# Sharing the opening loads of a layer-norm, state-space and GeGLU kernel among three issuing engines, and transposing x between the two halves of B

## The chip, the cores and the metric

The kernel runs on one core of a Trainium2 chip. In the profile, TensorE (matrix products, and here transposes too) is PE, its weight loads PEld, VectorE DVE, ScalarE ACT and GpSimd POOL; SyncE (SP) does nothing here but issue transfers (DMA). A q behind a name stands for that engine's sequencer, which here issues transfers or waits. TensorE's results go to PSUM buffers. The metric is the device time of one execution in microseconds (us), as the median of several. Each kernel also has a profile of one execution; its span is some 1.8 us shorter than that execution's time, because the time holds a little more than the instructions. All profiles used here are of fast executions; an execution is called slow when it lies over 1.5% above the fastest of the same kernel. Ratios compare one kernel's fast executions with those of the kernel before in the same rounds, so they are not quite the ratio of the medians that stand beside them. Landing records, and the times of single packets, were read from the trace file itself; they are not among the views shown.

## The reference, cut to what matters

Over 2048 tokens with 512 features: a layer norm, then two branches of the same normalised x, multiplied.

```python
xn = _layernorm(x, axis=-1)
# s: Bu = xn @ B_bar.T (complex B), h = Lam_bar * h + Bu over 2048 steps,
#    y = 2 * Re(h @ C.T) + xn * Dskip
s = _A_ref(xn, Lambda_re, Lambda_im, B_re, B_im, C_re, C_im, log_dt, Dskip)
# g: silu of a feed-forward of width 1376
g = _silu((_gelu(xn @ w_gate) * (xn @ w_up)) @ w_down)
return x + s * g
```

## The kernel before: the parts that matter

The tokens are worked on in four blocks of 512. TensorE needs x and B with the features on the partitions, so both have to be transposed. For block 0 this is done on TensorE at the very start, and that opening is what the change rewrites.

```python
for m in range(M):                                   # M = 4 pieces of x (0 to 3), 128 KB each
    nc.sync.dma_start(out=x_tok[:, m, :], in_=x_r[:, m, :])
for i, v in enumerate((A_log_dt, A_Lambda_im, A_Lambda_re, A_Dskip)):   # 1 KB each
    nc.scalar.dma_start(out=pv[4 * i : 4 * i + 4, :], in_=...)
for ri, src in enumerate((A_B_re, A_B_im)):          # 512 KB each
    nc.sync.dma_start(out=Bn[:, ri, :, :], in_=...)
# ... weights; identity and constants on GpSimd; "tiny", a first Sin on ScalarE ...
dummies(10)                 # matmuls on zeros, meant to have TensorE's clock up
# transpose of the parameters (pt_ps), dummies(3), statistics of x, norms 0 and 1
b_transposes(0)             # 16 transposes, two ScalarE copies
tps = [t_xn0(0, xs[0]), t_xn0(1, xs[1])]
xs += [norm0(2), norm0(3)]
b_transposes(1)
# copies of x's transposes 0, 1; transposes 2, 3; their copies; then the first products, u_ps
```

For blocks 2 and 3 the normalised x is transposed by DMA, one piece of 128 tokens at a time, while TensorE works on the block before. The change does not touch this code, but the explanation needs it:

```python
def ln_out(s, m):
    xn = work.tile([P, D], BF16, name="xn", tag="xn", bufs=4)
    ACT(out=xn[:], in_=x_tok[:, s * M + m, :], func=AF.Identity, ...)
    nc.sync.dma_start_transpose(out=xnT[:, :, c0 : c0 + P], in_=xn[:])
# in step j (of 11) of block s:
if 5 <= j < 5 + M:
    ln_out(s + 1, j - 5)    # the last piece is in step 8; the next block's u_ps follow step 10
```

## Time and profile before

| | kernel before |
|---|---|
| time, median of 3 (range) | 188.81 us (188.59 to 189.18) |
| span of the profile | 187.59 us |
| first product, u_ps of block 0 | 10.35 us |
| last block's first u_ps | 123.40 us |

The page's engine lines and the opening's chain of waits are in the prediction below. Two more things are worth a look. The first is the timeline of the opening (columns: start, length in us, engine, line, operation, tile; in brackets the idle time and what ended it):

```profile
2.94 1.29 DVE L151 BATCH_NORM_STATS2 st<-x_tok 128x6 f32<-128x512 bf16 x2 [1.82 <-DMA x_tok<-in_A_x_dram]
```

VectorE runs the statistics of the first two pieces of x back to back, so both had landed by 3.6. The second is the chain of waits just before the last block (start, length, what):

```profile
119.96 3.31 DMA xnT<-xn
...
123.40 4.69 PE u_ps L333 x21
```

Here the end of the kernel hangs on a transfer: the last piece of block 3's transposed x, issued at 119.96 and landed 3.31 us later.

### The profile page before, as it was taken

What the parts mean: (1) busy time and instruction counts of PE and PEld (TensorE: products, weight loads), DVE (VectorE), ACT (ScalarE), POOL (GpSimd) and SP (SyncE); (2) the same over time, 40 slices, a digit from 0 to 9 for tenths busy, and PEclk for the clock granted to TensorE, in tenths of its full rate; (3) what the DMA queues carried; (4) which work ended last, traced back from release to release, by engine and by line L of the source; (5) the groups of instructions that cost most, each with busy time, mean ns of one, the idle gap of its engine ahead of it and who ended that gap; (6) DMA issues with size and microseconds to landing.
All of it is one profiled execution on the core that took longest, in us unless ns stands there. A gap on an engine that the chain in (4) does not pass through costs nothing.

```text
span 187.6 us, 2592 instructions
## 1 busy us (share of the span) xinstructions
PE 180.8 (96%) x918; PEld 86.0 (46%) x918; DVE 156.0 (83%) x269; ACT 116.2 (62%) x209; POOL 21.2 (11%) x35
## 2 busy tenths in 40 slices
PE   7789999999999999999999999989999999999992
PEld 2644444444444444544444444544444444554452
DVE  4859999999999599999999997999999999332033
ACT  3499899997279969257259947937428733441210
POOL 3745400000000330000000192000000000000000
PEclk9999999999999999999999999999999999999999
DMA  5999968600000013200000001420000000000001
GB/s 145 330 365 361 225 123 246 119 3 0 0 0 0 0 30 86 56 28 28 3 2 0 2 0 42 101 56 28 0 0 0 3 0 28 28 29 31 28 28 58
DMA packets 21164, 12.26 MB, mean 65 GB/s; under 512 B 11456, under 2 KB 21152, under 8 KB 21152
## 3 DMA queue, kind: packets, MB, share of 16 engines
q1 hardware_dynamic: 20976, 12.03, 23.9%
q8 instruction: 7, 0.11, 0.2%
q10 hardware_dynamic: 176, 0.07, 0.1%
q14 instruction: 5, 0.04, 0.1%
HBM read 7.38 MB, written 2.10 MB: 51 GB/s over the span
## 4 chain that ended last, share of the span: by engine, by line
PE 57%; DVE 21%; ACT 10%; DMA 4%; POOL 3%; issue 3%; SPq 1%; POOLq 1%; ACTq 0%; DVEq 0%
PE f_ps L438 15%; PE u_ps L333 11%; PE g_ps L418 10%; PE up_ps L423 10%; PE y_ps L453 6%; DVE Ft L382 6%; ACT junk L508 3%; DVE qq L352 3%; ACT gt L428 3%; ACT ub L430 3%; DVE pp L352 3%; DVE Wt L356 2%; DMA Bn<-in_A_B_re_dram 2%; DMA xnT<-xn 2%; DVE at L431 1%
## 5 line engine op out<-in xcount | busy, mean ns | idle before, releaser
L418 PE MATMUL g_ps<-xnT,wg 128*128 128x512 bf16 (+1 forms) x176 | 45.2, 379 | 0.0
L423 PE MATMUL up_ps<-xnT,wu 128*128 128x512 bf16 (+1 forms) x176 | 45.2, 379 | 0.0
L438 PE MATMUL f_ps<-wd,at 128*128 128x512 bf16 (+1 forms) x176 | 38.7, 379 | 0.0
L428 ACT ACTIVATE gt<-g_ps 128x512 bf16<-128x512 f32 (+1 forms) x44 | 26.0, 592 | 10.0 <-PE g_ps L418 7.8
L382 DVE TENSOR_TENSOR_SCAN Ft<-rho,it,Wt 128x512 bf16<-128x512 f32 x24 | 29.9, 1271 | 0.0
L333 PE MATMUL u_ps<-xnT,BT 128*128 128x512 bf16 x128 | 28.3, 379 | 1.1 <-DVE xnT L212 0.6
L430 ACT ACTIVATE ub<-up_ps 128x512 bf16<-128x512 f32 (+1 forms) x44 | 26.3, 597 | 3.9 <-PE up_ps L423 3.8
L453 PE MATMUL y_ps<-C,hst 128*128 128x512 bf16 x120 | 28.3, 379 | 0.0
L423 PEld LDWEIGHTS <-wu 128*128 128x128 bf16 (+1 forms) x176 | 17.6, 100 | 20.4
L438 PEld LDWEIGHTS <-at 128*128 128x128 bf16 (+1 forms) x176 | 17.2, 98 | 20.6
L443 ACT ACTIVATE g<-f_ps 128x512 f32<-128x512 f32 x16 | 9.6, 597 | 27.1 <-PE f_ps L438 27.1
L418 PEld LDWEIGHTS <-wg 128*128 128x128 bf16 (+1 forms) x176 | 17.2, 100 | 18.4
L431 DVE TENSOR_TENSOR at<-gt,ub 128x512 bf16<-128x512 bf16 (+1 forms) x44 | 18.1, 414 | 7.3 <-ACT ub L430 7.1
L338 ACT ACTIVATE U<-u_ps 128x512 bf16<-128x512 f32 x32 | 17.8, 602 | 9.0 <-PE u_ps L333 9.0
L471 DVE TENSOR_TENSOR yg<-y_ps,g 128x512 bf16<-128x512 f32 x15 | 10.3, 684 | 13.7 <-PE y_ps L458 9.9
L333 PEld LDWEIGHTS <-BT 128*128 128x128 bf16 x128 | 12.3, 98 | 15.9 <-issue 1.4
L453 PEld LDWEIGHTS <-hst 128*128 128x128 bf16 x120 | 11.7, 98 | 13.6
L523 ACT ACTIVATE xn<-x_tok,nb,rs 128x512 bf16<-128x512 bf16 x12 | 9.7, 812 | 5.6 <-POOL nb L519 5.6
L513 POOL TENSOR_SCALAR sx<-sx 128x4 f32<-128x4 f32 x2 | 2.2, 1118 | 82.0 <-ACT junk L508 82.0
L356 DVE TENSOR_TENSOR Wt<-pp,qq 128x1024 bf16<-128x1024 bf16 x16 | 10.6, 688 | 0.3
L356 DVE TENSOR_TENSOR hst<-pp,qq 128x1024 bf16<-128x1024 bf16 x16 | 10.6, 687 | 0.2
L508 ACT ACTIVATE junk<-x_tok 128x512 bf16<-128x512 bf16 x16 | 10.1, 629 | 0.3
(109 smaller groups left out, 163.3 us busy)
## 6 DMA issues: line engine op xcount, KB each, us to landing
out_dram<-ot SPq DMA_DIRECT2D x15, 128.0 KB, 1.7
x_tok<-in_A_x_dram SPq DMA_DIRECT2D x3, 512.0 KB, 3.9
wd<-in_B_w_down_dram SPq DMA_DIRECT2D x1, 1280.0 KB, 10.5
x_tok<-in_A_x_dram SPq DMA_DIRECT2D x4, 128.0 KB, 2.2
Bn<-in_A_B_re_dram SPq DMA_DIRECT2D x1, 512.0 KB
Bn<-in_A_B_im_dram SPq DMA_DIRECT2D x1, 512.0 KB, 5.0
wg<-in_B_w_gate_dram SPq DMA_DIRECT2D x1, 512.0 KB, 9.4
wu<-in_B_w_up_dram SPq DMA_DIRECT2D x1, 512.0 KB
```

The source lines that it names most:

```text
L333: nc.tensor.matmul(u_ps[:, :], lhsT=BT[:, ri, kt, pt * P : (pt + 1) * P], rhs=xnT[:, kt, cols], start=(kt == 0), stop=(kt == KT - 1),)
L338: ACT(out=U[:, ri, q, :], in_=u_ps[:, :], func=AF.Copy)
L356: return lambda: TT(out=dst()[i], in0=box["pp"][:, i, :, :], in1=box["qq"][:, 1 - i, :, :], op=op)
L382: nc.vector.tensor_tensor_scan(out=box["F"][:, ri, q, :], data0=rho[:, pt : pt + 1].to_broadcast([P, TS]), data1=box["W"][:, ri, q, :], in ...
L418: nc.tensor.matmul(g_ps[:fs, :], lhsT=wg[:, kt, fsl], rhs=xnT[:, kt, cols], start=(kt == 0), stop=(kt == KT - 1))
L423: nc.tensor.matmul(u_ps[:fs, :], lhsT=wu[:, kt, fsl], rhs=xnT[:, kt, cols], start=(kt == 0), stop=(kt == KT - 1))
L428: ACT(out=gt[:fs], in_=g_ps[:fs, :], func=AF.Gelu_apprx_tanh)
L430: ACT(out=ub[:fs], in_=u_ps[:fs, :], func=AF.Copy)
L431: dve(now() + 0.9, 0.34, lambda: TT(out=at[:fs, j, :], in0=gt[:fs], in1=ub[:fs], op=ALU.mult))
L438: nc.tensor.matmul(f_ps[:, :], lhsT=at[:fs, k, m0 : m0 + P], rhs=wd[:fs, k, :], start=(k == 0), stop=(k == NFT - 1))
L453: nc.tensor.matmul(y_ps[:, :], lhsT=hst[:, j // NPT, j % NPT, m0 : m0 + P], rhs=C2[:, j // NPT, j % NPT, :], start=(j == 0), stop=False,)
L508: ACT(out=junk[:], in_=x_tok[:, s * M + m, :], func=f, accum_out=sx[:, s, i, m : m + 1])
```

## The change

Its intent: move ScalarE's table load to the front, spread the issues of the opening loads over three engines so that half of B comes sooner, and put the transposes of x where TensorE would wait for B's other half. Core of the diff:

```diff
+    tiny = consts.tile([P, 1], FP32, name="tiny")
+    ACT(out=tiny[:], in_=halfpi[:], func=AF.Sin)          # table load, now first on ScalarE
     for i, v in enumerate((A_log_dt, A_Lambda_im, A_Lambda_re, A_Dskip)):
-        nc.scalar.dma_start(out=pv[4 * i : 4 * i + 4, :], ...)
+        nc.gpsimd.dma_start(out=pv[4 * i : 4 * i + 4, :], ...)
-    for m in range(M): nc.sync.dma_start(out=x_tok[:, m, :], ...)      # (stood above)
-    for ri, src in enumerate((A_B_re, A_B_im)): nc.sync.dma_start(out=Bn[:, ri, :, :], ...)
+    nc.sync.dma_start(out=x_tok[:, 0, :], ...)
+    nc.sync.dma_start(out=x_tok[:, 1, :], ...)
+    nc.sync.dma_start(out=x_tok[:, 2:M, :], ...)
+    load_b(nc.scalar, 0, A_B_re)
+    load_b(nc.sync, 1, A_B_im)
 ...
-    dummies(10)
-    (transpose of the parameters pt_ps, dummies(3), statistics, copy pf, norms 0 and 1,
-     thn, a1, b_transposes(0), x transposes 0 and 1, norms 2 and 3, b_transposes(1))
+    dummies(12)
+    b_transposes(0)
+    (statistics, norms 0 and 1, x transposes 0 and 1, transpose of the parameters pt_ps,
+     b_transposes(1), copy pf, norms 2 and 3)
     (copies of x 0 and 1, x transposes 2 and 3, their copies)
+    (thn, a1)
 ...
-    clk["pe"] = 9.5
+    clk["pe"] = 9.3                                       # start assumed in the VectorE schedule
```

More of the change, by code (lines that the diff above doesn't have):

```diff
@@ L87, with load_b @@
     wu_r = B_w_up.rearrange("(k p) f -> p k f", p=P)
-    for m in range(M):
-        nc.sync.dma_start(out=x_tok[:, m, :], in_=x_r[:, m, :])
-    for i, v in enumerate((A_log_dt, A_Lambda_im, A_Lambda_re, A_Dskip)):
-        nc.scalar.dma_start(out=pv[4 * i : 4 * i + 4, :], in_=v.rearrange("(k p) -> k p", p=P))
-    for ri, src in enumerate((A_B_re, A_B_im)):
-        nc.sync.dma_start(out=Bn[:, ri, :, :], in_=src.rearrange("(k p) d -> p k d", p=P))
+    def load_b(eng, ri, src):
+        eng.dma_start(out=Bn[:, ri, :, :], in_=src.rearrange("(k p) d -> p k d", p=P))
+    halfpi = consts.tile([P, 1], FP32, name="halfpi")
+    nc.vector.memset(halfpi[:], math.pi / 2)
+    tiny = consts.tile([P, 1], FP32, name="tiny")
+    ACT(out=tiny[:], in_=halfpi[:], func=AF.Sin)
+    for i, v in enumerate((A_log_dt, A_Lambda_im, A_Lambda_re, A_Dskip)):
+        nc.gpsimd.dma_start(out=pv[4 * i : 4 * i + 4, :], in_=v.rearrange("(k p) -> k p", p=P))
+    nc.sync.dma_start(out=x_tok[:, 0, :], in_=x_r[:, 0, :])
+    nc.sync.dma_start(out=x_tok[:, 1, :], in_=x_r[:, 1, :])
+    nc.sync.dma_start(out=x_tok[:, 2:M, :], in_=x_r[:, 2:M, :])
+    load_b(nc.scalar, 0, A_B_re)
+    load_b(nc.sync, 1, A_B_im)
     cuts = [0, 3 * P, 7 * P, F]
@@ L107 @@
     nc.vector.memset(warm[:], 0.0)
-    halfpi = consts.tile([P, 1], FP32, name="halfpi")
-    nc.vector.memset(halfpi[:], math.pi / 2)
     ident_f = consts.tile([P, P], FP32, name="ident_f")
@@ L120 @@
     nc.gpsimd.memset(mhalf[:], -0.5)
-    tiny = consts.tile([P, 1], FP32, name="tiny")
-    ACT(out=tiny[:], in_=halfpi[:], func=AF.Sin)
     euler = consts.tile([P, NPT], FP32, name="euler")
@@ L181 @@
     ch = consts.tile(W3, BF16, name="ch")
-    dummies(10)
+    dummies(12)
+    b_transposes(0)
+    for a in (0, 2):
+        for m in (a, a + 1):
+            bn(0, m)
+        for m in (a, a + 1):
+            bn_end(0, m)
+        rstd(0, a, a + 2)
+    xs = [norm0(0), norm0(1)]
+    tps = [t_xn0(0, xs[0]), t_xn0(1, xs[1])]
     pt_ps = psum.tile([P, 16], BF16, name="pt_ps", tag="ps")
     nc.tensor.transpose(pt_ps[:, :], pv[:, :], ident[0:16, 0:16])
-    dummies(3)
-    bn(0, 0)
-    bn(0, 1)
-    bn_end(0, 0)
-    bn_end(0, 1)
-    rstd(0, 0, 2)
-    bn(0, 2)
+    b_transposes(1)
     nc.vector.tensor_copy(out=pf[:], in_=pt_ps[:, :])
     nc.gpsimd.tensor_tensor(out=dt_[:], in0=euler[:], in1=ldt, op=ALU.pow)
-    bn(0, 3)
-    bn_end(0, 2)
-    bn_end(0, 3)
-    rstd(0, 2, 4)
-    xs = [norm0(0), norm0(1)]
-    STT(out=thn[:], in0=lim, scalar=1.0 / (2.0 * math.pi), in1=dt_[:], op0=ALU.mult, op1=ALU.mult)
-    TT(out=a1[:], in0=lre, in1=dt_[:], op=ALU.mult)
-    nc.gpsimd.tensor_tensor(out=rho[:], in0=euler[:], in1=a1[:], op=ALU.pow)
-    b_transposes(0)
-    tps = [t_xn0(0, xs[0]), t_xn0(1, xs[1])]
     xs += [norm0(2), norm0(3)]
-    b_transposes(1)
     for m in range(2):
@@ L212 @@
         nc.vector.tensor_copy(out=xnT[:, :, m * P : (m + 1) * P], in_=tps[m][:, :, :])
+    STT(out=thn[:], in0=lim, scalar=1.0 / (2.0 * math.pi), in1=dt_[:], op0=ALU.mult, op1=ALU.mult)
+    TT(out=a1[:], in0=lre, in1=dt_[:], op=ALU.mult)
+    nc.gpsimd.tensor_tensor(out=rho[:], in0=euler[:], in1=a1[:], op=ALU.pow)
     TT(out=ang[:], in0=iota_f[:].unsqueeze(1).to_broadcast(W3), in1=thn[:].unsqueeze(2).to_broadcast(W3), op=ALU.mult)
```

## The prediction

> **What bounds the kernel now.** I read the page first: TensorE is busy for 96% of the span, so only the places where it is not busy, and the place where it starts, can be worth anything. The page's lines that say so:
>
> ```profile
> PE 180.8 (96%) x918; PEld 86.0 (46%) x918; DVE 156.0 (83%) x269; ACT 116.2 (62%) x209; POOL 21.2 (11%) x35
> PE   7789999999999999999999999989999999999992
> ```
>
> The reader is to see that the thin slices are the first two (4.69 us each) and the last. The change touches only what runs before the first real product, so I read next the chain that ended last, piece by piece, from 0 to 45 us (columns: start, length, what):
>
> ```profile
> 2.18 0.43 SPq L89
> 2.61 0.04 issue
> 2.65 4.07 DMA Bn<-in_A_B_re_dram
> 6.72 0.05 issue
> 6.77 1.07 PE tb_ps L140 x16
> 7.84 0.45 PE tp L171 x8
> 8.28 1.00 PE tb_ps L140 x16
> 9.28 0.24 PE tp L171 x4
> 9.52 0.02 issue
> 9.54 0.77 DVE xnT L212 x2
> 10.31 0.04 issue
> 10.35 7.07 PE u_ps L333 x32
> ```
>
> So the start is a chain: SyncE issues four pieces of x, then the real half of B; that half lands at 6.72; 32 transposes of B and 16 of the normalised x follow, two DVE copies end it, and at 10.35 the first product u_ps starts. From 10.35 to 52.9 the chain is TensorE without a gap. From 52.9 to 123.4 it goes through ScalarE and VectorE work that hangs on a product ending at 52.9, then back to TensorE. No piece of it starts at a fixed time of its own. A start later by d therefore ends the kernel later by about d.
>
> The other direction is not symmetric. The timeline near 36 us:
>
> ```profile
> 29.62 5.22 SPq L525 DMA_TRANSPOSE xnT<-xn  x4
> 36.30 6.59 PEld L333 LDWEIGHTS <-BT 128*128 128x128 bf16 x32 [0.36 <-DMA xnT<-xn]
> ```
>
> The second token block's transposed x arrives just when TensorE wants it: the weight load had sat idle for 0.36 us until that transfer, although TensorE itself ran on. SyncE's queue runs without a pause from 16.9 us (eight transposes of C, two loads of x, then these four), so this arrival is set by transfers. An earlier start gains only as far as the queue is earlier too.
>
> **What the Trainium skill says.** "DMA: Bandwidth & Descriptors", section "Issuing engines are not separate DMA queues": transfers started by ScalarE, SyncE or GpSimd run on the same 16 DMA engines and interleave; several issuers save only issue time. The trace before agrees as to the bound: from 4.4 to 7.2 us the DMA engines moved 349 to 367 GB/s with one queue doing nearly all of it, so a second queue has little left to add. The same page, "Queues, rings and completion order": each DMA engine takes turns between the queues that have work. No trace here shows that, since the second queue carried only 4 KB. "Perfetto Trace Analysis", section "DVE / Act Engine Instruction": an ACTIVATE is pushed into a wait queue, after which the sequencer is free for the next instruction. If a DMA issue runs on that sequencer, it could pass the table load. The trace before cannot settle that: there the four issues came first (until 2.27) and the load at 2.29. "DMA: Bandwidth & Descriptors", section "Anatomy of one DMA — SWDGE (gpsimd) path": a GpSimd transfer has descriptors written by software and about 2 us of fixed cost. No run here has one.
>
> **The change, part by part.**
>
> *ScalarE's table load* starts at about 0.75 instead of 2.29. It takes 1.28 and the first Sin 0.20, and ScalarE's next work was at 7.43: hidden both times, worth 0.
>
> *The loads.* Before, x (0.52 MB) moved until about 3.85, the rate fell to 91 GB/s until 4.40, and B_re followed. It moved by about 5.75 and landed at 6.72, so landing is 0.97 after the last byte. Afterwards SyncE issues three pieces of x (0.46 each, from 0.72) and B_im at about 2.1. If ScalarE's issue of B_re waits for load and Sin, it is at 0.75 + 1.28 + 0.20 = 2.25, only 0.4 earlier than the 2.65 before. B_im was issued 0.15 before it, and the two halves share the engines. Steady data for B_re began some 1.6 after its issue, so both flow from about 3.75. Two halves are 1.05 MB, at 357 GB/s 2.95 us: data until 6.7, landing at 7.65. B_re would be 0.9 later than now, B_im (needed at 8.21 before) 0.5 earlier. The saved issues and the filled dip (0.55 us at 91 instead of 350, about 0.4 us of transfer) go to the second half, which was not the one waited for.
>
> *GpSimd.* Four issues now come ahead of the identity and the constants. I take 1 us each, an estimate from the skill's fixed cost of 2 us, half of it held by GpSimd. The identity, ready at 1.65 before, would be at 5.7, the -0.5 vector at 6.3 and the first power (0.73) at 7.1. That is still ahead of a B_re landing at 7.65, and the parameters land at about 6.7, ahead of their use at 9.2.
>
> *The order after B_re lands*, at time L. TensorE: B_re transposes 1.07, eight x transposes 0.45, then the parameter transpose (0.18). DVE then has, in this order, the parameter copy 0.15 (which waits for it), two normalisations 0.74, two copies 0.75, two copies 0.77. With some 0.2 of hand-overs: L + 1.07 + 0.45 + 0.18 + 0.15 + 0.74 + 0.75 + 0.77 + 0.2 = L + 4.3. Before it was 10.35 - 6.72 = 3.63, because the two late normalisations (7.24) and first copies (8.10) ran beside the transposes. Now they queue behind the parameter copy, which is behind B_re. This costs about 0.65.
>
> *The angles.* thn and a1 (0.15 each) move behind the copies, so ScalarE's Sin, the wide cosine copy and the eviction of u_ps follow 0.3 later relative to TensorE. Eight PSUM buffers cover that; TensorE did not wait for ScalarE there before. Two dummy matmuls replace three: nothing, while TensorE waits for B_re anyway.
>
> Sum in this case: u_ps at 7.65 + 4.3 = 11.95, 1.6 later.
>
> **The rivals.**
>
> *The issue passes the table load.* B_re is issued at about 0.8 and shares with x. Both, 1.05 MB, flow from 1.95 (x's first bytes in the timeline of DMA) at some 340 GB/s until 5.05; x lands at 5.8 instead of about 4.8 (3.85 + 0.97), B_re at 6.0. Now x's statistics are late: the last pair of bn_stats, its closing and ve take 1.85, to 7.65; two normalisations to 8.4, transposes to 8.95, then parameters, two normalisations, four copies as above (2.6): 11.5, or 1.2 later. For it speaks the skill's lifecycle, against it nothing.
>
> *The intended gain.* B_re lands near 5.9 with x no later: 5.9 + 4.3 = 10.2, a gain of 0.15. For it speaks that the author moved the assumed start in the VectorE schedule from 9.5 to 9.3, and fewer dummies. Against it: 1.05 MB by 5.0 needs full rate from 1.95, and x's small pieces ran at 272 GB/s. Even a larger gain would be cut at 36 us to the queue's own, about 0.4.
>
> *GpSimd becomes the bound.* If its issues take 2 us each, the identity comes at 9.7 and everything follows it: some 13.5, 3 us later, just inside 2%.
>
> *A cold TensorE.* The dummies end near 5.1, and a wait until 7.65 is 2.5 us. If the clock dropped, the 3.2 us of transposes would lose up to another 2.
>
> **Range and chances.** I weigh the first case 45% (+1.6), the passing issue 30% (+1.2), the intended gain 25% (-0.1): about +1.0. 188.81 + 1.0 = 189.8 us. The intended gain to the limit at 36 us gives 188.4; a delayed GpSimd or a cold clock in part 191.4. 2% is 3.78 us; a gain of that size would need u_ps at 6.6, before any of B can be transposed. Slower by 2% needs a GpSimd catastrophe: 4%.
>
> **What would show it.** Right: B_re's transposes start after 7; normalisations 2 and 3 follow the parameter copy on DVE with no gap up to u_ps; u_ps starts at 11 to 12; the span grows by as much. Which case it is shows in where ScalarE's DMA issue lies against the table load. Wrong: u_ps before 10.35; GpSimd issues far from 1 us; a span that moves by much less than u_ps, which would mean the later chain has slack that I did not see.

## The result, and the profile after

The changed kernel took 190.72 us (median of 4, 190.64 to 190.80) against 189.0 us for the kernel before (median of 4, 188.59 to 189.28): a ratio of 1.0093, 95% interval 1.0071 to 1.0114. It is the same within 2%, but slower by 0.9% without doubt. The profiled span grew by 1.43 us, from 187.59 to 189.02.

Where did that arise? I took the start of the first u_ps of each block from the two traces:

| us | before | after | difference |
|---|---|---|---|
| first u_ps of block 0 | 10.35 | 11.12 | +0.77 |
| from there to the first of block 2 | 69.18 | 69.13 | -0.05 |
| from there to the first of block 3 | 43.87 | 44.57 | +0.70 |
| from there to the end | 64.19 | 64.20 | +0.01 |

So between these two profiles half of the loss is made in the opening, and the other half in a place that the change did not touch, more than 100 us later. (The blocks are numbered from 0; the expectations below call block 2 the third one.)

**The opening.** The page after, engine line and DMA queues (packets, megabytes, share of the 16 engines' time):

```profile
PE 180.6 (96%) x900; PEld 86.3 (46%) x917; DVE 156.0 (83%) x269; ACT 116.2 (61%) x209; POOL 23.7 (13%) x39
...
q10 hardware_dynamic: 672, 0.59, 1.0%
q8 instruction: 7, 0.11, 0.3%
```

TensorE is as busy as before, within 0.2 us. Queue q10, ScalarE's, had carried 0.07 MB; now it carries B_re. Queue q8 will matter further down. The timeline of the opening after:

```profile
0.72 1.28 ACT L94 ACT_TABLE_LOAD   x1 [0.72 <-PEq L610]
...
0.89 0.43 ACTq L89 DMA_DIRECT2D Bn<-in_A_B_re_dram  x1
...
4.96 0.69 DVE L155 BATCH_NORM_STATS2 st<-x_tok 128x6 f32<-128x512 bf16 x1 [1.32 <-DMA x_tok<-in_A_x_dram]
...
8.92 0.17 DVE L201 CAST pf<-pt_ps 128x16 f32<-128x16 bf16 x1 [0.60 <-PE pt_ps L199]
```

B_re is issued at 0.89, while the table load (0.72 to 2.00) is still running: "behind the table load" in the program is not behind it in time. So B_re now shares the DMA engines with x. In the trace's landing records (a transfer is cut over 16 DMA engines and has landed when the last of them reports) it landed at 4.73 instead of 6.72, but piece 1 of x landed at 4.93 instead of 3.35, and pieces 2 and 3 at 5.74 instead of 3.88 and 4.17. VectorE waited 1.32 us for piece 1. The chain of waits shows what this made of the opening:

```profile
1.18 3.75 DMA x_tok<-in_A_x_dram
...
4.96 0.69 DVE st L155
...
7.51 0.17 DVE ve L161
...
8.05 0.72 PE tp L175 x8
...
9.09 0.65 DVE xn L166 x2
9.74 0.67 DVE xnT L205 x2
10.40 0.67 DVE xnT L208 x2
...
11.12 0.39 PE u_ps L332
```

Before, this chain began with B_re and ran through TensorE. Now B is nowhere in it: it begins with x and stays on VectorE but for eight transposes and the parameters' transpose. The B_re that came 2 us sooner was of no use to anyone; its transposes began at 6.12, after twelve dummies, and TensorE then still waited 0.88 us for x.

**Before the last block.** The same stretch of the chain as shown of before:

```profile
120.66 4.12 DMA xnT<-xn
...
124.82 1.69 PE u_ps L332 x7
```

The same transfer takes 4.12 instead of 3.31, and in the timeline TensorE stands still for it:

```profile
124.82 2.55 PE L332 MATMUL u_ps<-xnT,BT 128*128 128x512 bf16 x10 [1.19 <-DMA xnT<-xn]
```

It waited 1.19 us here, and 0.50 before: a difference of 0.69, the whole +0.70. The landing records point to the reason. Of the 16 DMA engines, 15 had delivered their share by 123.10. The sixteenth delivered at 124.78. At 122.66 begins one packet of 16,384 bytes of queue q8, which took 1.06 us; the last two words of the transpose started only as it was done, at 123.71. The packet records that were kept do not name the DMA engine; that the packet lay on the sixteenth one is read from this timing. Queue q8 is the one that the page calls "instruction". It has seven such packets in each run, about one for every 260 TensorE instructions in the records, so I read it as TensorE's own program being fetched.

### The profile page after: what moved, and what is told of

Its sections match the earlier page's. It is cut to its first block, busy times and chain, and to the rows that moved or that the text cites. A ratio compares the mean times of both kernels' runs of the same rounds, so it can differ in the third digit from the quotient of the medians.

```text
span 189.0 us, 2574 instructions
## 1 busy us (share of the span) xinstructions
PE 180.6 (96%) x900; PEld 86.3 (46%) x917; DVE 156.0 (83%) x269; ACT 116.2 (61%) x209; POOL 23.7 (13%) x39
## 4 chain that ended last, share of the span: by engine, by line
PE 55%; DVE 23%; ACT 10%; DMA 4%; issue 3%; POOL 3%; POOLq 1%; SPq 0%; ACTq 0%; DVEq 0%
PE f_ps L437 15%; PE u_ps L332 11%; PE g_ps L417 10%; PE up_ps L422 10%; DVE Ft L381 6%; PE y_ps L452 6%; ACT junk L507 3%; DVE qq L351 3%; ACT gt L427 3%; ACT ub L429 3%; DVE pp L351 2%; DVE Wt L355 2%; DMA xnT<-xn 2%; DMA x_tok<-in_A_x_dram 2%; DVE at L430 1%
## 5 line engine op out<-in xcount | busy, mean ns | idle before, releaser
L417 PE MATMUL g_ps<-xnT,wg 128*128 128x512 bf16 (+1 forms) x174 | 44.7, 379 | 0.1
L452 PE MATMUL y_ps<-C,hst 128*128 128x512 bf16 x116 | 27.8, 379 | 0.1
```

What stands on the lines that cost most here:

```text
L417: nc.tensor.matmul(g_ps[:fs, :], lhsT=wg[:, kt, fsl], rhs=xnT[:, kt, cols], start=(kt == 0), stop=(kt == KT - 1))
L452: nc.tensor.matmul(y_ps[:, :], lhsT=hst[:, j // NPT, j % NPT, m0 : m0 + P], rhs=C2[:, j // NPT, j % NPT, :], start=(j == 0), stop=False,)
```

## The experiments

Two theories of the +1.4 us. **The opening alone**: everything later follows the first product, and a difference between profiles near 123 us is chance. **Opening and fetch**: about half is lost in the opening, and half because an instruction fetch lies on the last engine of one transfer. Within the opening, the question is what ScalarE's early issue of B_re costs or brings, and what the new order costs. All kernels gave correct results. Three executions were slow (191.47 of one experiment, 191.73 and 191.87 of the kernel before) and are not in the ratios. The kernel before beside the three groups of runs had medians of 189.19, 189.4 and 189.01 (11 each).

In this table, "fetch" is the start of the fifth q8 packet, counted from the first u_ps of block 2, and "block 2 to 3" is the time between the first u_ps of these blocks. Without a wait the latter is 43.22.

| kernel | first u_ps | fetch | block 2 to 3 | time, median | ratio |
|---|---|---|---|---|---|
| before | 10.35 | +40.44 | 43.87 | 188.81 | 1 |
| before, again | 10.59 | +44.11 | 43.22 | 189.01 | 0.9989 |
| before, one dummy fewer | 10.59 | +44.06 | 43.22 | 188.99 | 1.0007 |
| before, pairs | 11.27 | +39.89 | 43.22 | 189.32 | 0.9985 |
| before, three pieces, pairs | 10.38 | +40.01 | 43.22 | 188.98 | 0.9996 |
| after | 11.12 | +42.42 | 44.57 | 190.72 | 1.0093 |
| after, again | 11.90 | +42.38 | 44.42 | 191.16 | 1.0108 |
| after, one dummy more | 11.02 | +42.36 | 44.48 | 190.96 | 1.0097 |
| after, norms first | 10.99 | +42.59 | 44.65 | 190.54 | 1.0059 |
| after, B_re held | 14.01 | +42.42 | 44.50 | 193.55 | 1.0233 |
| after, B_re on SyncE | 10.64 | +42.69 | 44.73 | 190.65 | 1.0083 |
| the same, parameters on ScalarE | 11.27 | +40.51 | 43.90 | 189.22 | 0.9979 |
| after, nine small matmuls | 11.14 | +38.92 | 43.58 | 190.06 | 1.0056 |
| after, pairs | 11.27 | +39.75 | 43.22 | 189.54 | 1.0008 |

### Group 1: one more dummy, one fewer, B_re held back, B_re on SyncE

**One dummy matmul more in the kernel after.** If the fetch goes by a count of TensorE instructions, two more instructions (a matmul and its weight load) should move it.

```diff
-    dummies(12)
+    dummies(13)
```

> The changed kernel with 13 dummy matmuls instead of 12, so that TensorE's program has as many instructions ahead of every point as in the kernel before. Fetch theory: 0.65 us of the change's 1.7 us is lost at 123 us, because a 16 KB fetch of TensorE's own instructions (at 122.66, 1.06 us long) sat in one DMA engine ahead of the last word of the last transposed x; before, that fetch came at 119.96. With 13 dummies it should come near 120.7 again, the first product of the last block starts some 0.7 us sooner, ratio about 1.006. Rival (the whole loss comes from the start): ratio stays at 1.009. First product at 11.1 in both.

190.96 us (6 executions, ratio 1.0097, 1.0077 to 1.0118). The fetch stayed at +42.36, the wait stayed, and the time did not move. This was a miss: so small a shift of the count leaves the fetch where it is.

**One dummy fewer in the kernel before**, the mirror image:

```diff
-    dummies(3)
+    dummies(2)
```

> The kernel before with 12 dummy matmuls instead of 13, nothing else. Fetch theory: the start stays at 10.35, but the instruction fetch near 120 us moves to about 122 and delays the last block's first product by some 0.6 us: ratio about 1.003. Rival: a dummy less changes nothing, ratio 1.000.

188.99 us (6, ratio 1.0007, 0.9977 to 1.0037), another miss. The fetch did move, but to +44.06, after the last block had begun, where it held nothing up. The last transpose landed at 122.62, 2.43 after its issue, and TensorE did not wait. A later repeat of the kernel before did the same unchanged, so this movement cannot be credited to the dummy.

**B_re made to wait for the table load.** The first Sin writes one column of B's buffer, so that the load has to come after it. This makes the prediction's first case real.

```diff
-    ACT(out=tiny[:], in_=halfpi[:], func=AF.Sin)
+    ACT(out=Bn[:, 0, 0, 0:1], in_=halfpi[:], func=AF.Sin)
```

> The changed kernel, with B_re's issue made to wait for the Sin behind the table load (the Sin writes one column that the load then overwrites). So the order that the change's words describe is really held: issue at about 2.25 instead of 0.89. First case of the prediction: x lands by 4.6 (5.7 in the changed kernel), B_re at about 7.6, first product at about 11.9, ratio about 1.013. Rival (x's lateness is the only cause, B_re has slack): first product near 10.6, ratio about 1.006.

193.55 us (4, ratio 1.0233, 1.0212 to 1.0255). Its chain of waits:

```profile
2.25 6.48 DMA Bn<-in_A_B_re_dram
...
8.86 1.86 PE tb_ps L144 x16
10.73 0.85 PE tp L175 x8
```

The issue is at 2.25, as the prediction had it for its first case, but landing took until 8.73 rather than 7.65. The two halves of B share the engines, and there is a second price: 16 transposes take 1.86 here and 1.07 elsewhere. The windows (from:to, length, busy time and count of TensorE, weight loads, VectorE, ScalarE, GpSimd, then the granted TensorE clock, DMA share and GB/s):

```profile
8.00:8.80 0.80, 0.00 (x0) 0.00 (x0) 0.00 (x0) 0.00 (x0) 0.00 (x0) 0.97 1.10 363
8.80:9.50 0.70, 0.64 (x7) 0.67 (x8) 0.00 (x0) 0.00 (x0) 0.00 (x0) 0.50 1.10 348
```

TensorE had nothing to do for 2.87 us, and its clock was granted at 0.50 for 3.4 us, from 8.76 to 12.17 in the trace's clock records. The prediction's "cold TensorE" exists, then, but not in the profile of the changed kernel, where TensorE never waits a whole microsecond between its first dummy and the first product. Had its issue not passed the table load, the change would have cost 2.8 us more (193.55 against 190.72).

**B_re back on SyncE, behind x, everything else as after.**

```diff
-    load_b(nc.scalar, 0, A_B_re)
+    load_b(nc.sync, 0, A_B_re)
```

> The changed kernel with B_re on SyncE's queue between x and B_im, so that nothing shares the engines with x. Sharing theory: x lands by 4.6, B_re at about 6.2 (issued 0.55 sooner than before), normalisations at 6.4; then the parameter transpose is next: if the GpSimd-issued parameters land at about 8.4 as in the changed kernel, first product at 11.0 and little is gained (ratio 1.008); if they land by 7.6, first product at 10.4 and ratio about 1.004 with the fetch's 0.6 still in it.

190.65 us (6, ratio 1.0083, 1.0055 to 1.0112). Chain of waits:

```profile
2.11 4.62 DMA Bn<-in_A_B_re_dram
...
6.78 1.07 PE tb_ps L144 x16
...
10.64 0.39 PE u_ps L332
```

Pieces 2 and 3 of x land at 4.81 (5.74 in after, 4.17 at the latest before), and B_re is on the chain again. B_re is issued 0.54 sooner than before (2.11 against 2.65), because x goes out in three issues instead of four, and still lands where it did (6.73 against 6.72). The first u_ps comes 0.48 sooner than in the kernel after. The part that is left against before is the new order: 10.64 - 6.73 = 3.91 from landing to first product, against 3.63, so 0.28. In these three profiles the opening's +0.77 is thus 0.48 for the early issue of B_re and 0.29 for the order. These are single readings: the kernel before and its variants with the same opening code start at 10.35 to 11.27 in the table. And yet the time is as long as after's, as the fetch delays block 3 just as there (44.73). The opening alone cannot explain that.

### Group 2: parameters off GpSimd, pairs of transposes, norms first

**Also the parameters back on ScalarE**, to see whether GpSimd's small transfers keep B_re from landing:

```diff
-        nc.gpsimd.dma_start(out=pv[4 * i : 4 * i + 4, :], ...)
+        nc.scalar.dma_start(out=pv[4 * i : 4 * i + 4, :], ...)
-    load_b(nc.scalar, 0, A_B_re)
+    load_b(nc.sync, 0, A_B_re)
```

> As the run with both halves of B on SyncE behind x, but the four parameter vectors go on ScalarE's queue again (they pass the table load). GpSimd-queue theory: in that run B_re landed at 6.73 although it was issued 0.54 sooner than before, x's second piece at 4.07 instead of 3.35, and the parameters at 8.09, because some DMA engines were held up beside the GpSimd-issued transfers. With none of those, x lands as before or sooner, B_re at about 6.2, parameters by 5, and the first product starts at 10.1 to 10.3. Rival (the later landing comes from the data rate alone): B_re again at 6.7 and first product at 10.6. Time: ratio 0.999 to 1.003, depending on the last block's wait.

189.22 us (6, ratio 0.9979, 0.9945 to 1.0012). Chain of waits:

```profile
2.11 5.17 DMA Bn<-in_A_B_re_dram
```

B_re landed later, not sooner, so that idea fell. Of its 16 shares the eighth came at 5.91, the last at 7.27: the slowest DMA engines set the landing. What this run does show stands in the last columns of the table. Set beside the run above, its first product is 0.63 later and its median time is 1.4 us shorter. The profile is of this run's slowest execution (190.21), so the like-for-like figure is the span of the two profiles: 188.40 here, 188.71 there. The fetch lies at +40.51 here, and the wait before block 3 is about what it was before the change. The start of the first product is not what sets the order of these two kernels.

**Block transposes in pairs, in the kernel before and in the kernel after.** The last piece goes out one step earlier or more, ahead of need; a fetch on one of its engines should then cost nothing.

```diff
-                    if 5 <= j < 5 + M:
-                        ln_out(s + 1, j - 5)
+                    if 5 <= j < 5 + M // 2:
+                        ln_out(s + 1, 2 * (j - 5))
+                        ln_out(s + 1, 2 * (j - 5) + 1)
```

> The kernel before, with the x transposes of blocks 2 and 3 issued in two pairs instead of one per step, so that the last of them is issued some 0.8 us sooner (119.2 instead of 119.96) and is no longer behind an output store. Fetch theory: the last block's first product then does not wait for the transfer even where an instruction fetch delays one DMA engine by 1 us; it starts 43.2 after the block before it (43.87 in the kernel before), so the span falls by 0.6 us: ratio about 0.997. Rival: that wait is an accident of one profile and the runs without one are no slower: ratio 1.000.

> The changed kernel with the same pairing. Fetch theory: the last block's first product starts 43.2 to 43.5 after the block before it instead of 44.6; only the late start (0.77 us) remains, against the paired kernel before: ratio to the kernel before about 1.001, and 1.004 to the paired one. Rival (the change's whole 1.7 us is made elsewhere): ratio to the kernel before 1.006 or more.

Before with pairs: 189.32 us (6, ratio 0.9985, 0.9950 to 1.0020). After with pairs: 189.54 us (6, ratio 1.0008, 0.9979 to 1.0037); that is 1.2 us less than after by the medians, and 0.85% or 1.6 us by the ratios, at an opening that was in its profile even 0.15 later. With pairs in both kernels, 0.2 us (medians) or 0.4 us (ratios) of the change's loss are left. By the executions, then, the transfer before the last block seems to make up more than half of the loss, though the intervals of these ratios (0.3% either way) do not fix its share. The even split of the first two profiles came about because the profile of before has a wait of 0.65 us there itself (43.87 against 43.22), which its repeat below does not have. Chain of waits of after with pairs:

```profile
123.55 0.22 PE y_ps L457 x4
123.77 2.37 PE u_ps L332 x11
```

No transfer is left in it; TensorE runs through into block 3. The sixteenth share was still late (15 landed by 120.74, the last at 122.25, with a fetch from 120.14 to 121.22), only now 1.4 us ahead of need. Pairs also take the last piece out from behind an output store (120.03 in after, just ahead of the transpose at 120.66). That store is not what made the wait: in the kernel before with one dummy fewer it stands there too (119.57, the transpose at 120.19), and the transfer took 2.43. In the profiles, 44.57 became 43.22, that is 1.35 us, between the two. The kernel before gained nothing visible from the same edit, at a first product of 11.27 in its profile: B_re landed only at 7.69 there. That opening is the same code as before's, so it is run-to-run spread.

**Norms 2 and 3 ahead of the parameter copy on VectorE**, to price the term "order" of the prediction:

```diff
+    xs += [norm0(2), norm0(3)]
     pt_ps = psum.tile([P, 16], BF16, name="pt_ps", tag="ps")
     ...
-    xs += [norm0(2), norm0(3)]
```

> The changed kernel with the normalisations of x's last two pieces moved ahead of the parameter copy on VectorE. The prediction's order term: VectorE idled 0.60 us for the parameter transpose; without that the first product starts 0.3 to 0.4 us sooner, at 10.75 instead of 11.12; ratio about 1.007 against 1.009. Rival (x's late landing alone decides, and the copies wait for the transposes anyway): first product still at 11.1.

190.54 us (6, ratio 1.0059, 1.0029 to 1.0090). Chain of waits:

```profile
8.92 1.00 PE tb_ps L144 x16
9.92 0.24 PE tp L175 x4
...
10.18 0.77 DVE xnT L208 x2
```

Less than expected: the first product came 0.13 sooner. (The ratio is 0.3% lower than after's, but the two intervals overlap and the rounds differ.) VectorE's queue was shorter, but the second half of B now stood on the chain, between the first and the second pair of x transposes. Two paths of nearly the same length lie side by side here, and taking one away gave the difference between them, not its own length.

### Group 3: repeats, moving the fetch, and the best of both

**Both kernels again, unchanged**, for the spread of the profile readings.

> The kernel before once more, unchanged, for a second profile. Two theories on what varies: B_re's landing varies from run to run (6.72, 6.96 and 7.69 in three profiles with the same loads), so the first product may start anywhere from 10.3 to 11.3 here; and the instruction fetch near 120 us is fixed by the program, so it comes again 40.4 us after the third block's first product, with the last block's 43.9 after it. Rival: the fetch's place is random too. Ratio 1.000.

> The changed kernel once more, unchanged. Same theories: first product within 0.2 of 11.1 (it hangs on x, which has varied little), the fetch again 42.4 us after the third block's first product and the last block's first product 44.5 to 44.7 after it. Rival (the place is random): the fetch elsewhere, the wait between 43.2 and 44.7. Ratio 1.009.

Before: 189.01 us (4, ratio 0.9989, 0.9948 to 1.0030, called unclear). After: 191.16 us (4, ratio 1.0108, 1.0073 to 1.0143). In the repeat of before the fetch was at +44.11, not +40.44, and there was no wait (43.22), so the fetch's place is not fixed by the program alone. In the repeat of after it was at +42.38 again. The opening of the repeat of after was 0.78 later still, for a reason of its own:

```profile
3.04 6.31 DMA pv<-in_A_Dskip_dram
...
9.49 0.18 PE pt_ps L199
...
11.90 0.39 PE u_ps L332
```

The last parameter vector, 1 KB on GpSimd's queue, landed 6.31 us after its issue, behind the large loads, and became the bound. In the profile of after with pairs it was the bound as well, landing at 8.73. In the first profile of after it landed at 8.42 and was just not the bound. So the parameters on GpSimd are a risk of some 0.8 us that the first profile does not show.

**Nine small matmuls more (16 columns each) after the twelve dummies.** They shift TensorE's instruction count by 18 and its time hardly at all.

```diff
-    dummies(12)
+    dummies(12, 9)      # nine more matmuls on 16 columns, in the same PSUM tile
```

> The changed kernel with nine 16-column matmuls after the 12 dummies: 18 more instructions for TensorE and some 0.3 us of work while it waits for x anyway. Fetch theory: the fetch comes 18 instructions sooner, at about 40.4 us instead of 42.4 after the third block's first product, the last block's wait shrinks to that of the kernel before (43.9), ratio about 1.005. Rival: 44.6 again, ratio 1.009.

190.06 us (6, ratio 1.0056, 1.0029 to 1.0084). Now the fetch moved, further than expected, to +38.92, in front of the last transpose's issue. Chain of waits:

```profile
121.38 2.42 DMA xnT<-xn
...
123.84 1.68 PE u_ps L334 x7
```

The transfer takes 2.42 instead of 4.12, with all 16 shares in at 123.80, at the same opening (11.14). Block 2 to 3 takes 43.58, 0.99 less than after, and the time is 0.7 us less (1.1 us less than the repeat of after in the same rounds, whose opening was 0.76 later in its profile). Against 43.22 there is 0.36 left: 0.20 of it is a wait for this transfer, which was issued 0.7 later than in after. That delay goes with the fetch too. It now lies (119.19 to 120.23) on the second of the block's four transposes: 15 of its shares landed by 119.77 and the sixteenth at 121.29, and SyncE's issues of the second and third took 3.29 instead of 2.62:

```profile
117.37 3.29 SPq L526 DMA_TRANSPOSE xnT<-xn  x2
```

The late share went with the fetch from the fourth transpose to the second, and the fourth transfer became as short as in the profiles without a wait (2.42, against 2.43). The code near 123 us is the same in both kernels. So the fetch is what made the wait. That 18 more TensorE instructions moved six of the seven q8 packets forward, by 1.4 to 3.5 us at an unchanged first product, also speaks for reading them as TensorE's program.

**The kernel before with x in three pieces and pairs of transposes**, the parts that looked good.

```diff
-    for m in range(M):
-        nc.sync.dma_start(out=x_tok[:, m, :], in_=x_r[:, m, :])
+    nc.sync.dma_start(out=x_tok[:, 0, :], in_=x_r[:, 0, :])
+    nc.sync.dma_start(out=x_tok[:, 1, :], in_=x_r[:, 1, :])
+    nc.sync.dma_start(out=x_tok[:, 2:M, :], in_=x_r[:, 2:M, :])
 ...                      (and ln_out in pairs, as above)
```

> The kernel before with x's block in three pieces instead of four and with the paired transposes of blocks 2 and 3; nothing else of the change. B_re is issued at 2.11 instead of 2.65: landing some 0.4 sooner, first product near 10.0 where no DMA engine lags, and the last block starts 43.2 after the third. Ratio about 0.995; if B_re's landing hangs on the slowest DMA engine rather than on its issue, 0.998.

188.98 us (6, ratio 0.9996, 0.9968 to 1.0024): not shown to be faster. Its profile has the shortest span of all, 186.87, and a chain that explains why the earlier issue is worth so little:

```profile
2.16 4.63 DMA Bn<-in_A_B_re_dram
...
7.49 2.87 ACT BT L144 x3
...
10.38 0.38 PE u_ps L334
```

B_re's eighth share landed at 5.71, its last at 6.79. Then ScalarE's copies of B's transposes (three at 0.96 each) are the bound, beside VectorE's copies at much the same time.

## Why the prediction was right or wrong

The time (190.72) lies in the predicted range and "within 2%" was right. The central value, 189.8, was 0.9 us too low. That it came so near is luck in part: its +1.0 was the mean of three openings (+1.6, +1.2 and -0.1), none of which is the measured +0.77, and nearly half of the measured +1.43 arose where the prediction expected nothing. Point by point:

- **That a start later by d ends later by d** is the step that failed. It held from the first product to block 2 and from block 3 to the end, to 0.1 us in the table. In between, the start's +0.77 became +1.42. The prediction said of that stretch that it goes through ScalarE and VectorE "then back to TensorE" and left out its last link, a DMA transpose with almost no slack. Its landing depends on where an instruction fetch lies: 0.70 of the 1.43 us, and 1.35 against a profile without a wait.
- **Which case.** The prediction gave 45% to an issue that waits for the table load and 30% to one that passes it. It passed, at 0.89 against 0.72 to 2.00. That rival was right in its mechanism and in most of its sizes: x landed at 5.74 (predicted 5.8), the statistics were done at 7.68 (7.65), the x transposes at 8.77 on the chain (8.95). Two of these hits are near by chance: VectorE was busy from piece 1's landing at 4.93 on, so it is that piece and not x's last that set 7.68; and the rival has x landing "about 4.8" before, where the landing records have 4.17. One term was mis-sized: "parameters, two normalisations, four copies (2.6)" measured 2.3 from 8.77 to 11.08. Work back to back on VectorE adds 0.65 to 0.67 a pair to the chain, less than the 0.73 to 0.77 that a pair shows as busy, and hand-overs were 0.02 to 0.05. Hence 11.12 and not 11.5, +0.77 and not +1.2. B_re landed at 4.73, not 6.0, but was not on the path.
- **The first case, when forced**, was too kind: B_re landed at 8.73 instead of 7.65, and the half clock that the prediction put among its rivals followed the wait.
- **The term "order", +0.65,** measured 0.28 where B_re sets the start as before (and 4.00 - 3.63 = 0.37 in the run with the parameters on ScalarE). It was too large because of the same adding of overlapping durations.
- **GpSimd.** Predicted 1 us per issue, with half of the skill's 2 us held by GpSimd as its own assumption; measured 0.79, then 0.53 and twice 0.52. The identity was ready at 4.51, not 5.7, and nothing waited for it. But the parameters landed at 8.42 and, in the repeat, at 9.35, not 6.7. That they could become the bound themselves was not seen.
- **The limit at 36 us** was never tested, as no version started early enough.
- **Its own signs.** "Normalisations 2 and 3 follow the parameter copy with no gap" and "u_ps at 11 to 12" were right; "B_re's transposes start after 7" was wrong (6.12, when the dummies ended, which the prediction had "near 5.1"); "the span grows by as much" was wrong, and that sign pointed at the failed step.

What stays open is what places the fetch. With the parameters on GpSimd and the pairs and small matmuls left out, it lay at +42.36 to +42.69 in six profiles of six kernels or repeats; in the unchanged kernel before it lay at +40.44 once and +44.11 once. A count of TensorE's instructions does not settle it alone: moving the parameters from GpSimd to ScalarE left TensorE's program as it was, and the fetch went from +42.69 to +40.51. Nor is it shown, for lack of a trace of each, that the unprofiled executions of after all had the wait; the 1.2 us that pairs took off the median, against 1.35 between the profiles, suggests that most did.

## What to carry to other kernels

Before moving a load forward, ask who shares the DMA engines with it: an early load that nobody can use yet delays the one that is waited for. In a long chain, look for transfers that land just as they are wanted, because a small disturbance of one of 16 engines there adds to the end in full; issuing them a step earlier took 1.2 us off the changed kernel. And when two nearly equal paths lie side by side, shortening one is worth only their difference.

## What the Trainium skill lacked or had wrong

- "Runtime: NRT & Kernel Launch", section "Instruction fetch mechanics", has the refill in blocks of 16 KiB on the engine's own DMA queue and calls its cost "mostly hidden". The packets are there (seven of 16,384 bytes, 0.96 to 1.32 us each in the profile of after). It lacks that a fetch can delay a data transfer: 15 shares landed by 123.10, the sixteenth at 124.78, and TensorE stood still for 1.19 us. In these profiles the packets that I read as fetches are on q8.
- "Perfetto Trace Analysis", section "DVE / Act Engine Instruction": the freed sequencer is confirmed, but the page does not say that a DMA issue overtakes a table load ahead of it in the program. Here it was issued at 0.89, during a load from 0.72 to 2.00.
- "DMA: Bandwidth & Descriptors", section "Anatomy of one DMA — SWDGE (gpsimd) path", gives about 2 us of fixed cost. Behind other loads, 1 KB from GpSimd took 3.9 to 5.4 us from issue to landing in one profile and up to 6.31 in another.
- "TensorE: Matmul & The Clock Gate", section "What's actually happening", has the clock halved after at least one idle window of about 3.4 us. Here less was enough: the last dummy ended at 6.00, and the clock record goes to 0.50 at 8.76, 2.76 us later.
- "DMA: Bandwidth & Descriptors", section "Why a DMA increments its semaphore by 16 and not by 1", has that the up to 16 engines of one transfer finish independently. It gives no size for the spread in a large load: B_re's eighth and last shares landed at 5.71 and 6.79 in one profile and at 5.91 and 7.27 in another, 1.1 to 1.4 us apart, where an earlier issue had gained 0.5 us.
